# Outputs of a soft mixture of experts from C's stacked parts alone, nine first halves in one row, the last weights sent by halves

## The chip, the cores and the metric

One core of a Trainium2 chip. The metric is device time in microseconds for one execution of the whole program. Several runs of one kernel are taken and the median is given.

## The reference

The first stage is decayed block attention over `q, k, v` (4 batches, 8 heads, 768 positions, head size 64). Its result is reshaped to `x` with 3072 rows and 512 columns. The second stage is a soft mixture of 8 experts with 4 slots each, so 32 slots:

```python
logits = x @ phi                       # (3072, 32)
d = softmax of logits over the rows    # dispatch
slot_input = d.T @ x                   # (32, 512)
for e in range(8):                     # 4 slots each, F = 1024
    slot_out[e] = relu(slot_input[e] @ w1[e]) @ w2[e]
c = softmax of logits over the slots   # combine, "C" below
return c @ slot_out                    # (3072, 512)
```

All inputs and outputs are float32. The weights `w1` and `w2` are 16.8 MB each, the output is 6.3 MB.

## The kernel before, in words

The rows are cut into 24 tiles `t` of 128. In the first 110 us a loop over the tiles does the attention, the logits and the running softmax over rows, and accumulates the slots' inputs; meanwhile the weights `w1` (in "slabs" of 1 MB) and a first part of `w2` (tiles `w2t` of 256 KB, 2 KB pieces per partition) are loaded. Then the kernel closes the softmax with the last tile (lines 567 to 620), and runs the experts.

**Order.** Every engine takes its instructions in the order of the program text; a helper (line 53 of the profile) records all of them, so one line number stands for everything and groups are told apart by their tiles. All loads and outputs are issued by SyncE, one after the other, on one DMA queue.

**Experts.** `first(Q)` (lines 633 to 661) does `w1` for four experts (Q is 0 or 1): 64 matmuls into two banks, a relu on ScalarE and VectorE, then two VectorE transposes that make `hz[Q]`, the left operand of all `w2` matmuls of that Q. `second(part, ...)` (lines 676 to 690) does `w2` for one half of the contraction: 16 steps `n`, each a `quad` of 4 matmuls (8 records, because a float32 matmul runs as two passes). Steps 0 to 7 use `hz[0]`, steps 8 to 15 use `hz[1]`. `second(0)` yields the first 256 columns of the slots' outputs (the first half), `second(1)` the other 256. In `second(1)`, steps 12 to 15 use the last four units of weights (experts 4 to 7, 2 MB): steps 12 and 13 their rows with i = 0, steps 14 and 15 those with i = 1. A dictionary `fill` says before which steps other work is put in (`PUTS`, line 32).

**C.** `shares()` runs in the middle of `first(0)`. It ends the combine softmax and makes `parts`, C transposed in 32x32 blocks, as a rounded high part and a low part. `stack` (line 724) spreads these two over 128 partitions for eight tiles at a time, by 16 casts; three stacks cover the 24 tiles. Stacks 1 and 2 use ScalarE, GpSimd and VectorE in turn, stack 3 GpSimd alone. `CR` (lines 711 to 716) is a plain float32 copy of C for tiles 0 and 1.

**Outputs.** `take` copies a finished half of the slots' outputs from PSUM (first 128 columns on ScalarE, the others on VectorE). `spread` replicates it over the partitions by one matmul, and rounds it into a high and a low part (ScalarE, then VectorE on half of the partitions). `put(t, half)` makes one half of the columns for two tiles: two matmuls into one of five banks, a 128x512 copy to SBUF alternating between ScalarE and VectorE, and a DMA. For `t < 2 * SPLIT` each half is sent by itself (256 KB, 1 KB pieces); for the others one DMA of 512 KB goes after the second half. The pair t = 0 uses `CR` and needs no `spread`.

Of the kernel before, what the change touches and what calls it, by code (L numbers as in the profile page):

```python
# [8 lines left out]
F32 = mybir.dt.float32  # L9
# [5 lines left out]
P = 128  # L15
B, H, S, DH = 4, 8, 768, 64
NB = S // P
T = B * NB
HP = H // 2
D = H * DH  # L20
SL = 32
# [7 lines left out]
FS = (0, 0)  # L29
HD = D // 2  # L30

PUTS = ((2, (0, 1)), (6, (2,)), (8, (2,)), (10, (2,)))
SPLIT = 7
PACE = 76
AHEAD = 40

# [22 lines left out]
def decay_attn_soft_moe(  # L59
# [13 lines left out]
    pe, dve, act, pool, sp = (InOrder(tc, x) for x in (nc.tensor, nc.vector, nc.scalar, nc.gpsimd, nc.sync))  # L73

    const = ctx.enter_context(tc.tile_pool(name="const", bufs=1))
    slabs = ctx.enter_context(tc.tile_pool(name="slabs", bufs=NSLAB))
# [6 lines left out]
    def bank(tag):  # L83
        return ps.tile([P, 512], F32, tag=tag, name=tag)
# [17 lines left out]
    wt = {}  # L102
# [3 lines left out]
    units = [(Q, 4 * part + 2 * m, q) for part in range(2) for Q in range(2) for m in range(2) for q in range(4)]  # L106
    single = [(Q, x, q, i) for Q, x, q in units[:NONE] for i in range(2)]
    single.reverse()
    units = units[NONE:]
# [6 lines left out]
    def load_one(pool_, tag, bufs):  # L116

        Q, x, q, i = single.pop()
        t_ = pool_.tile([P, 512], F32, tag=tag, name="w2t", bufs=bufs)
        sp.dma_start(out=t_, in_=rows(Q, x, q)[i])  # L120
        wt["w2", Q, q, x, i] = t_

    def load_two():

        (Q, x, q), other = units.pop(), units.pop()
        assert other == (Q, x, q + 1)
        t_ = slabs.tile([P, 2, 2, 512], F32, tag="slab", name="w2p")
        src = w2[4 * Q + q:4 * Q + q + 2, x:x + 2].rearrange("e x p d -> e (x p d)")
        sp.dma_start(
            out=t_.rearrange("p e i d -> p e (i d)"), in_=src.rearrange("e (p y) -> p e y", p=P)  # L130
        )
        for n in range(2):
            for i in range(2):
                wt["w2", Q, q + n, x, i] = t_[:, n, i, :]
# [12 lines left out]
    half = []  # L147

    def half_slab(name):

        if not half:
            t_ = slabs.tile([P, 2, 1024], F32, tag="slab", name=name)
            half.extend([t_[:, 1], t_[:, 0]])
        return half.pop()
# [21 lines left out]
    ident = const.tile([P, P], F32, name="ident")  # L176
# [8 lines left out]
    for hh in range(2):  # L185
        for hp in range(HP):
            x = hh * HP + hp
            dve.tensor_tensor_scan(
                out=mask[:, hh, hp, :],
# [24 lines left out]
    e = const.tile([P, P], F32, name="e")  # L214
    d = const.tile([P, P], F32, name="d")
# [3 lines left out]
    AT, XT, X, ST, QS, KD = {}, {}, {}, {}, {}, {}  # L219
# [349 lines left out]
    for hp in range(HP):  # L569
        pe.matmul(  # L570
            out=pr[:, 0:P],
            lhsT=phi4[hp // 2][:, hp % 2].rearrange("p g s -> p (g s)"),
            rhs=XT[T - 1][:, hp, :],
# [8 lines left out]
    el = e  # L582
# [2 lines left out]
    wgt = small.tile([P, 1], F32, tag="alpha", name="alpha")  # L585
    act.activation(out=wgt, in_=negm, func=AF.Exp, bias=new, scale=-1.0)
    slots(G - 1)
    tr = bank("tr")
    for hp in range(HP):
        pe.transpose(tr[:, hp * P:(hp + 1) * P], XT[T - 1][:, hp, :], ident)  # L590
    xl = keep.tile([P, D], F32, tag="x", name="x", bufs=5)
    selw = small.tile([P, SL], F32, tag="selw", name="selw", bufs=1)
    act.activation(out=selw, in_=sel, func=AF.Copy, scale=wgt)
    act.copy(out=xl[:, 0:HD], in_=tr[:, 0:HD])
    dl = bank("dp")
    pe.transpose(dl[:, 0:P], el, ident)
    dn = small.tile([P, SL], F32, tag="dn", name="dn", bufs=1)
    dve.tensor_copy(out=dn, in_=dl[:, 0:SL])
    dve.tensor_copy(out=xl[:, HD:D], in_=tr[:, HD:D])

    si = bank("xa")
    for first_, (w_, x_) in ((True, (selw, acc)), (False, (dn, xl))):
        for n in range(4):
            pe.matmul(
                out=si[SL * n:SL * n + SL, 0:P].rearrange("p (i a r) -> p i a r", i=4, a=4),
                lhsT=w_,
                rhs=x_.rearrange("p (h a k r i) -> p h k i a r", h=2, a=4, k=2, i=4)[:, n // 2, n % 2],
# [25 lines left out]
    def first(Q, between=None):  # L633
        ph = [bank("gl"), bank("xb")] if Q == 0 else [bank("xa"), bank("tr")]
        split = "p (g x c) -> p x g c"
        for n in range(4):
            for j in range(2):
                for b in range(4):
                    w_ = wt["w1", Q, 2 * (b % 2) + j, n // 2][:, n % 2]
                    w_ = w_.rearrange(split, x=2, c=2 * P)[:, b // 2]  # L640
                    pe.matmul(
                        out=ph[j][SL * b:SL * b + SL, :].rearrange("p (g c) -> p g c", c=w_.shape[2]),
                        lhsT=sT[:, n, :],
                        rhs=w_,
                        start=(n == 0),
                        stop=(n == 3),
                    )
            if between is not None and n == 1:
                between()
        if Q == 1:  # L650
            hz.append(half_slab("hz").rearrange("p (a b) -> p a b", b=SL))
        h = half_slab("h").rearrange("p (j c) -> p j c", j=2)
        r_ = rown[:, 2 * Q:2 * Q + 2]
        act.activation(out=h[:, 0], in_=ph[0], func=AF.Relu, scale=r_[:, 0:1])
        dve.tensor_scalar(out=h[:, 1], in0=ph[1], scalar1=r_[:, 1:2], scalar2=0.0, op0=ALU.mult, op1=ALU.max)

        for i in range(2):
            dve.transpose(
                out=hz[Q][:, 16 * i:16 * i + 16].rearrange("p a b -> p (a b)"),
                in_=h.rearrange("p j (g r i) -> p i g j r", g=16, i=2)[:, i],  # L660
            )
# [33 lines left out]
        load_one(keep, "x", 5)  # L695
    load_one(keep, "xt", 4)
    load_one(keep, "x", 5)
    parts, CR = [], []

    def shares():  # L700

        denominators()
        lp = bank("dp")[:, 0:P]
        pe.transpose(lp, L, ident)
        for x in slot_softmax(G - 1, lp):
            pass
        for _ in range(2):
            parts.append(half_slab("part")[:, 0:T * SL].rearrange("p (t s) -> p t s", t=T))
        dve.transpose(out=parts[1], in_=CN)
        act.copy(out=parts[0].bitcast(F32R), in_=parts[1])  # L710
        CR.append(half_slab("CR")[:, 0:2 * P].rearrange("p (t c) -> p t c", t=2))
        for n in range(16):
            b, c = divmod(n, 4)
            r = slice(SL * b, SL * b + SL)
            copy = (act.copy, pool.tensor_copy, dve.tensor_copy)[n % 3]
            copy(out=CR[0][SL * c:SL * c + SL, :, r], in_=parts[1][r, 0:2, :])

    first(0, shares)
    for _ in range(4):
# [2 lines left out]
    CT, cts = [], []  # L722

    def stack(engines):

        x = len(CT)
        if x % 2 == 0:
            cts.append(slabs.tile([P, 2, 8, P], F32R, tag="slab", name="ct"))
        ct = cts[-1][:, x % 2]
        CT.append(ct)  # L730
        for n, (b, c) in enumerate((b, c) for b in range(4) for c in range(4)):
            r = slice(SL * b, SL * b + SL)
            src = parts[c % 2][r, 8 * x:8 * x + 8, :].bitcast(F32R)
            engines[n % len(engines)](out=ct[SL * c:SL * c + SL, :, r], in_=src)

    stack((act.copy, pool.tensor_copy, dve.tensor_copy))
    stack((act.copy, pool.tensor_copy, dve.tensor_copy))
    first(1)
    stack((pool.tensor_copy,))
    s4_ = cts[-1][:, 1].rearrange("p t c -> p (t c)")  # L740
    while units:
# [2 lines left out]
    so = work.tile([P, D], F32, tag="at", name="so", bufs=2)  # L744
# [3 lines left out]
    s4 = []  # L748
# [12 lines left out]
    def take(half, bank_):  # L761

        x = so[:, half * HD:(half + 1) * HD]
        act.copy(out=x[:, 0:P], in_=bank_[:, 0:P])
        dve.tensor_copy(out=x[:, P:HD], in_=bank_[:, P:HD])

    ow = {}

    def put(t, half):
        if half == 0:  # L770
            ow[t] = half_slab("o").rearrange("p (i c) -> p i c", i=2)
        o = ow[t]
        pf = bank(obanks[nput[0] % len(obanks)])
        for i in range(2):
            c_ = CT[t // 8][:, t % 8:t % 8 + 2] if t else CR[0]
            pe.matmul(
                out=pf[:, i * HD:(i + 1) * HD],
                lhsT=c_.rearrange("k t p -> k (t p)").rearrange("k (p i) -> k i p", i=2)[:, i],
                rhs=s4[half] if t else so[:, half * HD:(half + 1) * HD],
                start=True,  # L780
                stop=True,
            )
        copy = act.copy if nput[0] % 2 == 0 else dve.tensor_copy
        copy(out=o[:, :, half * HD:(half + 1) * HD], in_=pf.rearrange("p (i c) -> p i c", i=2))
        nput[0] += 1
        cols = slice(half * HD, half * HD + HD)
        if t >= 2 * SPLIT:
            cols = slice(0, D)
            if half == 0:
                return  # L790
        dst = out[t * P:(t + 2) * P, cols]
        sp.dma_start(out=dst.rearrange("(p i) c -> p i c", i=2), in_=o[:, :, cols])

    pairs = [(t, 0) for t in range(0, 2 * SPLIT, 2)] + [(0, 1)]
    pairs += [(t, 0) for t in range(2 * SPLIT, T, 2)]
    pairs += [(t, 1) for t in (*range(2 * SPLIT, T, 2), *range(2, 2 * SPLIT, 2))]
    pairs.reverse()

    def give(n):
# [10 lines left out]
    fill = {}  # L810
    for n, x in PUTS:
        fill[n] = lambda x=x: [split() if y == 0 else give(y) for y in x]
# [62 lines left out]
```

## Time and profile before

| What | Value |
|---|---|
| Median of 3 runs | 167.37 us (166.79 to 169.35) |
| Profiled execution | 167.14 us, of which the span of instructions is 165.3 us |
| Moved by DMA | 61.82 MB, mean 374 GB/s |
| Busy | TensorE 90%, VectorE 55%, GpSimd 43%, ScalarE 35% of the span |

Times in the views count from the span's start. PE is TensorE's matmul side and PEld its weight loads, DVE VectorE, ACT ScalarE, POOL GpSimd, SP SyncE. A busy PE is not PE at its peak. The DMA share is that of all 16 DMA engines together; it can read slightly over 1 in a short window, because a packet is counted where it starts.

### The profile page before, as it was taken

To read this page: it belongs to the slowest core of one execution; us is meant where nothing else is said; L and a number is where in the kernel's file an instruction comes from. 1 tells how busy PE (TensorE), PEld (TensorE's weight loads), DVE (VectorE), ACT (ScalarE), POOL (GpSimd) and SP (SyncE) were. 2 spreads that over 40 slices of the span, in tenths; PEclk is the share of its full clock that TensorE was granted. 3 is DMA by queue.
4 is the path that set the end of the run, shared out by engine and by line. 5 is a ranking of instruction groups with operands and counts; after the bars stand their busy time and mean duration, and the time that the engine had idled before them with its cause. 6 is when DMAs were issued, how large, how long until landed. Compare 5 with 4: busy or idle time off the path is not lost.

```text
span 165.3 us, 6275 instructions
## 1 busy us (share of the span) xinstructions
PE 149.1 (90%) x2651; PEld 109.0 (66%) x2651; DVE 90.3 (55%) x208; ACT 58.5 (35%) x147; POOL 71.8 (43%) x108
## 2 busy tenths in 40 slices
PE   6999999999989999999999999998999989989400
PEld 6778878677868878788868896863323455648300
DVE  2964445447744574568655775564388821328600
ACT  3134412443443444231635152242055902226400
POOL 2786790277447227766119665300022894000000
PEclk9999999999999999999999999999999999999955
DMA  5999999999999999999999999999999999982897
GB/s 165 357 418 392 312 363 414 410 423 401 412 416 402 417 409 408 410 350 344 402 415 401 415 391 394 404 390 367 375 336 396 418 416 423 396 302 76 362 402 251
DMA packets 25131, 61.82 MB, mean 374 GB/s; under 512 B 2576, under 2 KB 6288, under 8 KB 23056
## 3 DMA queue, kind: packets, MB, share of 16 engines
q1 hardware_dynamic: 24960, 61.42, 96.6%
q8 instruction: 21, 0.34, 0.7%
q14 instruction: 6, 0.05, 0.1%
q10 hardware_dynamic: 144, 0.01, 0.1%
HBM read 55.12 MB, written 6.29 MB: 371 GB/s over the span
## 4 chain that ended last, share of the span: by engine, by line
PE 66%; DVE 9%; DMA 5%; ACT 5%; POOL 4%; issue 3%; DVEq 0%; POOLq 0%; ACTq 0%
PE xa L53 17%; PE sc L53 14%; PE kv L53 10%; PE xb L53 8%; PE gl L53 8%; PE tr L53 7%; DMA w2t<-w_x 3%; DVE o L53 3%; ACT ct L53 2%; DVE mask L53 2%; DMA lam_sb<-lam_x 2%; POOL kd L53 2%; PE dp L53 2%; POOL qs L53 1%; DVE hz L53 1%
## 5 line engine op out<-in xcount | busy, mean ns | idle before, releaser
L53 DVE TENSOR_TENSOR at<-sc,mask 128x512 f32<-128x512 f32 x46 | 29.6, 685 | 15.4 <-PE sc L53 14.6
L53 ACT COPY x<-tr 128x512 f32<-128x512 f32 (+1 forms) x24 | 13.9, 578 | 37.7 <-PE tr L53 37.7
L53 POOL TENSOR_TENSOR qs<-ld,qpow 128x512 f32<-128x512 f32 x20 | 25.5, 1275 | 2.1 <-POOL kd L53 2.1
L53 PE MATMUL sc<-ld 64*64 64x128 f32 x736 | 26.0, 276 | 0.1
L53 PEld LDWEIGHTS sc<-ld 64*64 64x64 f32 x736 | 20.3, 133 | 6.2 <-issue 3.4
L53 POOL TENSOR_TENSOR dec<-st,qpow 128x256 f32<-128x256 f32 x16 | 9.9, 621 | 25.6 <-DVE st L53 25.5
L53 POOL TENSOR_TENSOR kd<-kn,mask 128x512 f32<-128x512 f32 x10 | 10.6, 1058 | 12.8 <-ACT kn L53 12.4
L53 PE MATMUL xa<-at,ld 128*64 128x128 f32 x192 | 15.8, 284 | 0.0
L53 DVE TENSOR_TENSOR st<-dec,kv 128x256 f32<-128x256 f32 x16 | 6.7, 422 | 16.5 <-PE kv L53 15.1
L53 PE MATMUL tr<-ident,xt 128*128 128x128 f32 x96 | 15.4, 283 | 0.0
L53 PE MATMUL xb<-at,ld 128*64 128x128 f32 x192 | 14.6, 273 | 0.1
L53 PE MATMUL xa<-qs,st 64*64 64x128 f32 x160 | 14.0, 274 | 0.7 <-POOL qs L53 0.3
L53 PE MATMUL xb<-qs,st 64*64 64x128 f32 x160 | 13.1, 274 | 0.6 <-issue 0.6
L53 PE MATMUL kv<-ld,kd 128*64 128x64 f32 x320 | 12.9, 223 | 0.1
L53 PEld LDWEIGHTS tr<-ident,xt 128*128 128x128 f32 x96 | 10.4, 141 | 3.8 <-issue 3.8
L53 POOL CAST ct<-part 32x256 fp32r<-32x256 f32 x26 | 10.3, 395 | 5.0 <-DVE part L53 3.9
L53 PEld LDWEIGHTS xa<-at,ld 128*64 128x64 f32 x192 | 10.0, 136 | 3.7 <-issue 1.6
L53 PEld LDWEIGHTS kv<-ld,kd 128*64 128x64 f32 x320 | 11.9, 138 | 0.8 <-issue 0.5
L53 PEld LDWEIGHTS xa<-qs,st 64*64 64x64 f32 x160 | 9.9, 133 | 3.0 <-issue 1.9
L53 PEld LDWEIGHTS xb<-at,ld 128*64 128x64 f32 x192 | 11.0, 137 | 0.3 <-issue 0.2
L53 POOL TENSOR_TENSOR kd<-ld,mask 128x512 f32<-128x512 f32 x10 | 10.6, 1059 | 0.0
L53 PEld LDWEIGHTS xb<-qs,st 64*64 64x64 f32 x160 | 9.4, 133 | 0.2 <-ACT xt L53 0.2
(148 smaller groups left out, 233.8 us busy)
## 6 DMA issues: line engine op xcount, KB each, us to landing
slab<-w_x SPq DMA_DIRECT2D x16, 1024.0 KB, 8.4
w2p<-w_x SPq DMA_DIRECT2D x10, 1024.0 KB, 10.6
ld<-qT SPq DMA_DIRECT2D x24, 256.0 KB, 6.8
ld<-kT SPq DMA_DIRECT2D x24, 256.0 KB, 6.5
ld<-vN SPq DMA_DIRECT2D x24, 256.0 KB, 7.5
w2t<-w_x SPq DMA_DIRECT2D x24, 256.0 KB, 5.4
y<-o SPq DMA_DIRECT2D x14, 256.0 KB, 4.0
ld<-kN SPq DMA_DIRECT2D x10, 256.0 KB, 7.2
```

What stands on the lines that cost most here:

```text
L53: return self._tc.keep_in_program_order(f(*args, **kwargs))
```

## The change

1. `PUTS` and `SPLIT`: in `second(1)`, `spread` of the first half stands before step 8 (was 2), and nine first halves (t = 0, 2, ..., 16) in one row before step 12 (were seven, spread over steps 2, 6, 8 and 10).
2. Nine pairs are sent by halves (were seven). The order after the last weights is (18, 0), spread of the second half, then second halves mixed with the two halves of t = 18, 20 and 22.
3. The pair t = 0 uses the stacked parts as all others do; `CR` and its 16 copies go.
4. The last four units of weights are loaded as two DMAs of 1 MB by i (pieces of 2 KB), where they were two DMAs by expert pairs (pieces of 4 KB).
5. `first(1)` stands between the first and the second stack (was after the second).
6. `take` is one ScalarE copy of 256 columns.
7. In the closing of the softmax the last tile is transposed into two banks instead of one, and the transpose of `el` is put ahead of it.

```diff
-PUTS = ((2, (0, 1)), (6, (2,)), (8, (2,)), (10, (2,)))
-SPLIT = 7
+PUTS = ((8, (0,)), (12, (9,)))
+SPLIT = 9
...
+    def load_four():
+        Q, x, _ = units[-1]
+        units.clear()
+        for i in range(2):
+            t_ = slabs.tile([P, 4, 512], F32, tag="slab", name="w2p")
+            src = w2[4 * Q:4 * Q + 4, x:x + 2].rearrange("e x p d -> e (x p d)")
+            sp.dma_start(out=t_, in_=src.rearrange("e (p i d) -> i p e d", p=P, i=2)[i])
+            for q in range(4):
+                wt["w2", Q, q, x, i] = t_[:, q]
+
     def load_two():
+        if len(units) == 4:
+            return load_four()
...
     slots(G - 1)
-    tr = bank("tr")
+    dl = bank("dp")
+    pe.transpose(dl[:, 0:P], el, ident)
+    tr = [bank(x) for x in ("tr", "sc1")]
     for hp in range(HP):
-        pe.transpose(tr[:, hp * P:(hp + 1) * P], XT[T - 1][:, hp, :], ident)
+        pe.transpose(tr[hp // 2][:, hp % 2 * P:(hp % 2 + 1) * P], XT[T - 1][:, hp, :], ident)
...
-    act.copy(out=xl[:, 0:HD], in_=tr[:, 0:HD])
-    dl = bank("dp")
-    pe.transpose(dl[:, 0:P], el, ident)
+    act.copy(out=xl[:, 0:HD], in_=tr[0][:, 0:HD])
...
-    dve.tensor_copy(out=xl[:, HD:D], in_=tr[:, HD:D])
+    dve.tensor_copy(out=xl[:, HD:D], in_=tr[1][:, 0:HD])
...
-        CR.append(half_slab("CR")[:, 0:2 * P].rearrange("p (t c) -> p t c", t=2))
-        for n in range(16):
-            b, c = divmod(n, 4)
-            r = slice(SL * b, SL * b + SL)
-            copy = (act.copy, pool.tensor_copy, dve.tensor_copy)[n % 3]
-            copy(out=CR[0][SL * c:SL * c + SL, :, r], in_=parts[1][r, 0:2, :])
...
     stack((act.copy, pool.tensor_copy, dve.tensor_copy))
+    first(1)
     stack((act.copy, pool.tensor_copy, dve.tensor_copy))
-    first(1)
     stack((pool.tensor_copy,))
...
-        act.copy(out=x[:, 0:P], in_=bank_[:, 0:P])
-        dve.tensor_copy(out=x[:, P:HD], in_=bank_[:, P:HD])
+        act.copy(out=x, in_=bank_[:, 0:HD])
...
-            c_ = CT[t // 8][:, t % 8:t % 8 + 2] if t else CR[0]
+            c_ = CT[t // 8][:, t % 8:t % 8 + 2]
...
-                rhs=s4[half] if t else so[:, half * HD:(half + 1) * HD],
+                rhs=s4[half],
...
-    pairs = [(t, 0) for t in range(0, 2 * SPLIT, 2)] + [(0, 1)]
-    pairs += [(t, 0) for t in range(2 * SPLIT, T, 2)]
-    pairs += [(t, 1) for t in (*range(2 * SPLIT, T, 2), *range(2, 2 * SPLIT, 2))]
+    pairs = [(t, 0) for t in range(0, 2 * SPLIT + 2, 2)]
+    ends = [(t, half) for t in range(2 * SPLIT, T, 2) for half in range(2)][1:]
+    for t in range(0, 2 * SPLIT, 2):
+        pairs += [(t, 1), *ends[:1]]
+        del ends[:1]
```

## Rows read from the trace of the kernel before

**Rows 1.** The page's 40 slices: busy tenths of TensorE and of the DMA engines.
```profile
PE   6999999999989999999999999998999989989400
...
DMA  5999999999999999999999999999999999982897
```

**Rows 2.** Waits, 115 to 156 us: who waited for whom, total, times, longest.
```profile
PE kv L53 <- DVE hz L53: 0.9, 1, 0.9
```

**Rows 3.** Chain of waits after 140 us: start, duration, what.
```profile
144.80 2.77 PE xa L53 x48
```

**Rows 4.** Stretches: length, busy time by engine, PE clock, DMA share, GB/s.
```profile
98.00:112.00 14.00, 13.84 (x243) 10.28 (x240) 8.44 (x27) 5.45 (x17) 4.87 (x6) 1.00 1.03 395
128.00:142.00 14.00, 13.10 (x206) 7.48 (x202) 6.39 (x13) 5.71 (x14) 9.28 (x24) 1.00 1.03 418
148.00:153.50 5.50, 5.11 (x32) 4.64 (x33) 4.09 (x8) 3.31 (x7) 0.00 (x0) 1.00 0.22 75
153.50:159.50 6.00, 1.10 (x8) 0.86 (x7) 2.09 (x4) 1.46 (x3) 0.00 (x0) 0.83 1.02 420
160.00:163.50 3.50, 0.00 (x0) 0.00 (x0) 0.00 (x0) 0.00 (x0) 0.00 (x0) 0.50 1.09 383
```

**Rows 5.** SyncE's issues in order: start, duration; last weights, then four outputs' issues.
```profile
128.16 0.43 SPq L53 DMA_DIRECT2D w2p<-w_x  x1
...
139.53 0.64 SPq L53 DMA_DIRECT2D y<-o  x1
...
150.13 0.53 SPq L53 DMA_DIRECT2D y<-o  x1
...
161.30 0.59 SPq L53 DMA_DIRECT2D y<-o  x1
```

**Rows 6.** DMA issues, the same four: KB, us from issue to landing.
```profile
w2p<-w_x SPq DMA_DIRECT2D x1, 1024.0 KB, 17.2
...
y<-o SPq DMA_DIRECT2D x1, 256.0 KB, 6.5
...
y<-o SPq DMA_DIRECT2D x1, 256.0 KB, 2.4
...
y<-o SPq DMA_DIRECT2D x1, 256.0 KB, 3.1
```

**Rows 7.** DMA queues, 143.6 to 144.6 us: packets, and those under a size.
```profile
DMA packets 362, 0.38 MB, mean 383 GB/s; under 512 B 24, under 2 KB 350, under 8 KB 362
```

**Rows 8.** Timeline, 112 to 113 us: start, duration, engine, instruction.
```profile
112.14 0.37 ACT L53 COPY x<-tr 128x256 f32<-128x256 f32 x1
...
112.55 0.42 DVE L53 COPY x<-tr 128x256 f32<-128x256 f32 x1
```

**Rows 9.** Timeline, 122 to 139 us, casts of C and the relu behind them.
```profile
122.32 1.51 ACT L53 COPY CR<-part 32x64 f32<-32x64 f32 x6
...
126.91 11.39 POOL L53 CAST ct<-part 32x256 fp32r<-32x256 f32 x26 [3.93 <-DVE part L53]
...
131.04 0.75 DVE L53 TENSOR_SCALAR hz<-tr,rown 128x512 f32<-128x512 f32 x1
```

**Rows 10.** Timeline, 136 to 144 us, matmuls of second(1) and the work put in.
```profile
136.35 1.05 PE L53 MATMUL xa<-w2p,hz 128*32 128x256 f32 x16
...
137.86 1.03 PE L53 MATMUL tr<-so,CR 128*128 128x256 f32 x4
...
142.36 0.51 PE L53 MATMUL dp<-ct 128*128 128x256 f32 x2
...
143.05 1.07 PE L53 MATMUL xa<-w2p,hz 128*32 128x256 f32 x16
```

**Rows 11.** Timeline, 147 to 151 us, what stands between the last weights and the outputs.
```profile
147.90 0.29 DVE L53 COPY so<-xa 128x128 f32<-128x128 f32 x1 [2.53 <-ACT so L53]
...
149.85 0.37 ACT L53 CAST ct<-xb 128x256 fp32r<-128x256 f32 x1 [1.99 <-PE xb L53]
...
150.12 0.59 ACT L53 COPY o<-dp 128x512 f32<-128x512 f32 x1
...
150.25 0.43 DVE L53 TENSOR_TENSOR ct<-xb,ct 64x256 fp32r<-64x256 f32 x1
```

More of the change, by code (lines that the diff above doesn't have):

```diff
@@ L697, in decay_attn_soft_moe @@
     load_one(keep, "x", 5)
-    parts, CR = [], []
+    parts = []
     def shares():
```

## The prediction, made before the changed kernel was run

> **What bounds the kernel now.** I read the page's slices first [rows 1]: TensorE and the DMA engines are both at nine tenths almost throughout, and the DMA row alone has a hole, the 2 in the fourth slice from the end. The stretches size it [rows 4]: from 148 to 153.5 us the DMA engines are busy for 0.22 of the time, so 0.78 x 5.5 = 4.3 us of transfer time is lost; before it they move 418 GB/s, behind it 420 and then 383. The end is the DMA queue's: the last output is issued at 161.30 and lands 3.1 us later, at 164.4 [rows 5, 6], 0.9 us ahead of the span's end at 165.3.
>
> The hole comes from the order of the work. The last weights land at 128.16 + 17.2 = 145.4 us [rows 5, 6]; TensorE runs its last 48 matmul records until 147.57 [rows 3]; then come take, the pair from CR, spread and its rounding [rows 11], and the queue runs dry meanwhile, with seven first halves as its only stock. After the second half of t = 0 at 150.13 five first halves follow that send nothing, hence a second dry stretch before 153.5.
>
> One more reading decides the size. Between 143.6 and 144.6 us 350 of 362 packets are under 2 KB [rows 7]: nearly all lanes of the queue already carry outputs (1 KB pieces), though the last weights land a microsecond later. A few DMA engines lag the others, and a transfer has landed only when the slowest lane has. The first output lands at 139.53 + 6.5 = 146.0 [rows 5, 6], 0.6 us behind the last weights, though it was issued 6.5 us earlier. So the slowest lane sets the end, and I count along it.
>
> **Prices on that lane.** A half of 256 KB at 383 GB/s takes 0.68 us, a whole of 512 KB at 420 GB/s 1.25 us [rows 4]. A check on before: 145.4 + 14 x 0.68 + 5 x 1.25 = 161.2 with a queue that never runs dry, and 164.4 is measured, so the hole costs this lane 3.2 us.
>
> **The change, part by part.**
>
> *Nine halves as stock, second halves mixed with the rest.* Eighteen halves and three wholes take 12.24 + 3.75 = 16.0 us, against 15.8 before: 0.2 us more. The stock of nine lasts on the slow lane until 145.4 + 9 x 0.68 = 151.5 us. The first second half must be there by then. From the last landing: 16 records of steps 14 and 15 at 2.77 / 48 each, 0.93 us [rows 3]; take as one ScalarE copy of 256 columns, 0.37 by the copy of that shape [rows 8]; the spread's matmuls, 0.6 at most (half of the float32 group of four at 1.03, and a start [rows 10]); rounding 0.37 + 0.43 [rows 11]; two matmuls 0.35, half of the 0.69 that two puts take [rows 10]; a copy of 0.59 [rows 11]; with 0.2 of hand-overs, 3.85 us. It is issued at 149.3 and lands, as a lone output does, 2.4 us later [rows 6], at 151.7; its place in the row would let it land at 152.2. It is in time by 0.5 us. Behind it the two copying engines finish a put every 0.3 us or so (0.59 on ScalarE beside a similar one), faster than 0.68. The hole on the slow lane closes: minus 3.2.
>
> *Weights by halves.* The queue then reads 2 MB in 2 KB pieces. The nearest row is the stretch from 98 to 112 us, where the w2t loads with such pieces move 395 GB/s, against 418 with 4 KB [rows 4]: 5.3 us against 5.0, plus 0.3. The other end is 0, because that stretch also holds other loads and small ones. Below nothing is excluded: larger pieces were not slower. I take 0.3, the row's own figure. In exchange steps 12 and 13 may start 2.5 us earlier than steps 14 and 15.
>
> *The nine puts in one row.* In front of step 12 they take TensorE 9 x 0.3 = 2.7 us, paced by the copies. Two puts take 0.69 where they interrupt the weights [rows 10], so 3.1 is the upper end. With the gains below, step 8 starts near 139.7 (its weights are 2 MB ahead of the last and land by 140.4 at the latest), the row at about 141.5 to 142.3, its end is at 144.3 to 145.4; steps 12 and 13 follow until 145.3 to 146.3. The lower end is hidden by the last landing at 145.7; the upper end delays the second half by 0.6, which is the margin above. SyncE issues nine sends at about 0.6 [rows 5], 5.4 us from 142.6 on, ahead of the slow lane throughout. Cost on the path 0, upper end 0.3.
>
> *CR goes, first(1) ahead of stack 2.* Now the relu of first(1) stands behind the casts on VectorE and ScalarE (131.04 [rows 9]), though its matmuls are done at about 128.5, and TensorE waits 0.9 us for hz [rows 2]. Without the CR copies (1.5 us on ScalarE [rows 9]) and with stack 2 behind it, hz comes about 2 us earlier; the wait goes, and what is late next is the weights' landing, so no more than 0.9 can be had. The pair from CR took TensorE 1.03 us [rows 10] against 0.3 now. TensorE thus reaches step 8 over 1 us earlier, but steps 14 and 15 wait for the landing at 145.4 + 0.3. These savings are cover for the row, and buy nothing by themselves. Stack 2's casts have until about 142.5; stack 3's stay on GpSimd, which does its 26 casts by 138.3 now [rows 9].
>
> *take on one engine* saves the serial 0.3 us of VectorE [rows 11] less 0.1. *The closing chain* loses the wait of VectorE's copy for ScalarE's [rows 8]; VectorE is busy with the slots' sum until shortly before, so 0.1 at best. Both lie ahead of the landing or inside the margin: 0.
>
> **Sum.** Last landing: 145.4 + 0.3 + 12.24 + 3.75 = 161.7. With the 0.9 behind it the span is 162.6, which is 165.3 - 3.2 + 0.2 + 0.3. The profiled execution takes 167.14 for a span of 165.3, so 1.84 more: **164.4 us**. Its own time is 0.2 below the median shown, which I leave.
>
> One rule speaks against sending more by halves. The rows say 0.68 us per half in a row, and so 0.2 us for four more. The Trainium skill, page "DMA: Bandwidth & Descriptors", section "Rules for kernel authors", wants at least 1 MiB per DMA, and its section "Bandwidth" gives 1 MB 78% and 64 KB 32% of the peak. By that rule the sum would grow; the 383 GB/s of the row of halves do not bear it out, and its case is the third rival.
>
> **Rivals.**
>
> 1. *The slow lane lags less, or 2 KB pieces cost nothing.* Then the common lanes decide: they idle until the first second half, which starts about 0.7 ahead of its landing at 151.7, and then need 9 x 0.68 + 3 x 1.25 = 9.9: last landing 160.9, span 161.8, time 163.6. With the lag but no price for pieces it is 164.1. For it: the lag is seen in one execution. Against: it is there at the last weights and at the first output alike. Chance 0.32.
> 2. *The hole is moved, not closed.* If TensorE comes to steps 14 and 15 late (row of nine at its upper end, a bank held by a copy) or VectorE is held at the (18, 0) copy in front of the rounding, each microsecond past the 0.5 of margin is lost: one to two of them give 165.4 to 166.4. Against: 0.9 + 0.7 us of TensorE's own savings. Chance 0.10.
> 3. *Small sends do not overlap.* A lone half takes 2.4 us; if four halves cost 4 x 2.4 = 9.6 where two wholes cost 2 x (2.4 - 0.68 + 1.25) = 5.9, that is 3.7 in place of 0.2: 167.9. The page named above would put it so. Against: fourteen halves already follow each other at 383 GB/s. Chance 0.03.
> 4. *The load by halves is slow, and the kernel slower.* The last two DMAs gather 2 KB pieces of four experts. At half the rate (209 GB/s) 2 MB take 10.0 us, 5 more: everything behind moves, and 164.1 becomes 169.1. It is slower than before once the rate falls below 2.1 MB / (5.0 + 3.0) us = 260 GB/s, and by 2% below some 190. Against: w2t has such pieces at 395 [rows 4]. Chance 0.05.
>
> **Numbers.** The forecast has 0.50, in 164.0 to 164.9. Two per cent, about what a measurement of this kernel can tell from no change, is 3.3 us, so 164.0 on the median and just under 163.9 on the profiled execution: the line cuts through rival 1 and touches the forecast. Faster: 0.27 of rival 1 and 0.10 of the forecast, 0.37. Slower: 0.04, nearly all of rival 4. Same: 0.59. The range of 162.9 to 166.2 takes in rival 1 with some gain on top and rival 2; it leaves out rivals 3 and 4.
>
> **What would show it.** Right: DMA share near 1 from 143 to about 161 us on the slow lane, a dip on the others of well under 2 us near 150; halves landing 0.7 us apart; TensorE waiting for w2p in front of step 14 and no longer for hz; last weights landing at 145 to 146. Wrong: a stretch without outputs after 148 (rival 2), weights landing after 147 (rival 4), halves over 0.8 us apart (rival 3), or weights and outputs landing without a lag (rival 1).

## The result, and the profile after

The changed kernel takes 166.23 us in the median of 22 runs, against 167.74 for 22 runs of the kernel before. The ratio is 0.990, interval 0.988 to 0.993: 1% faster, where 164.4 us and about 1.7% were forecast. Ratios leave out runs over 1.5% above the fastest of the same kernel, here among them one of 474.51 us. The profiled execution takes 166.88 us, with a span of 165.0.

The stretches behind the last weights first (columns as in [rows 4]), and below them the longest one in the kernel before.

```profile
142.50:145.00 2.50, 2.50 (x21) 2.05 (x16) 1.36 (x3) 1.57 (x3) 0.00 (x0) 1.00 0.22 85
149.00:150.50 1.50, 0.96 (x8) 0.96 (x9) 0.60 (x2) 0.44 (x2) 0.00 (x0) 1.00 0.49 168
142.50:154.00 11.50, 10.15 (x87) 7.54 (x82) 7.28 (x13) 7.31 (x14) 0.00 (x0) 1.00 0.79 284
```

```profile
142.50:154.00 11.50, 10.64 (x107) 7.95 (x108) 6.08 (x11) 5.23 (x11) 0.00 (x0) 1.00 0.63 226
```

The old hole from 148 to 153.5 [rows 4] is nearly gone: what is left of it is half a share between 149 and 150.5. But a new one stands in front of it. From 142.5 to 145 us the DMA engines are busy for 0.22 of the time, where the kernel before was already sending outputs [rows 7]. Over the whole stretch the idle time fell from 0.37 x 11.5 = 4.3 us to 2.4.

SyncE's issues of the changed kernel tell why, with start and duration, the last weights first and then the first, third, fourth, seventh, tenth and last output (read as [rows 5]).

```profile
128.32 4.02 SPq L53 DMA_DIRECT2D w2p<-w_x  x1
...
144.01 0.64 SPq L53 DMA_DIRECT2D y<-h  x1
...
145.39 0.59 SPq L53 DMA_DIRECT2D y<-o  x1
...
146.08 0.59 SPq L53 DMA_DIRECT2D y<-o  x1
...
148.10 1.54 SPq L53 DMA_DIRECT2D y<-o  x1
...
151.08 0.59 SPq L53 DMA_DIRECT2D y<-h  x1
...
159.51 0.58 SPq L53 DMA_DIRECT2D y<-o  x1
```

The same issues from start to landing, in the same order (read as [rows 6]).

```profile
w2p<-w_x SPq DMA_DIRECT2D x1, 1024.0 KB, 18.0
...
y<-h SPq DMA_DIRECT2D x1, 256.0 KB, 3.0
...
y<-o SPq DMA_DIRECT2D x1, 256.0 KB, 3.0
...
y<-o SPq DMA_DIRECT2D x1, 256.0 KB, 4.6
...
y<-o SPq DMA_DIRECT2D x1, 256.0 KB, 4.6
...
y<-h SPq DMA_DIRECT2D x1, 256.0 KB, 3.6
...
y<-o SPq DMA_DIRECT2D x1, 256.0 KB, 4.4
```

The first output goes out at 144.01, 4.5 us later than before (139.53 [rows 5]). From then on a half follows each 0.67 us or so, just the pace at which the queue drains, so that no stock is built. The first output lands at 147.0, 0.7 us behind the last weights at 146.3: the lane that set both had no hole, the others had. The third output lands at 148.4, the fourth at 150.7, 2.3 us later in place of 0.68; this document calls such a step the **jump**. The second half of t = 0 is issued at 151.08.

TensorE's part of it is in the chain of waits of the changed kernel (start, duration, what).

```profile
125.75 15.20 DMA w2p<-w_x
140.96 0.04 issue
141.00 1.92 PE xa L53 x28
142.92 0.44 PE tr L53 x2
...
145.56 1.91 PE xa L53 x32
147.47 0.02 issue
147.49 0.38 ACT so L53
...
147.91 0.71 PE xb L53 x2
...
148.65 0.38 ACT ct L53
...
149.06 0.44 DVE ct L53
...
149.54 0.51 PE tr L53 x2
```

Step 8 waits for its weights until 140.96; the row of nine starts at 142.92 only and ends at 145.5; steps 12 to 15 end at 147.47. The wait for hz [rows 2] is gone, and the waits (who for whom, total, times, longest) now show weights in its place:

```profile
PE xa L53 <- DMA w2p<-w_x: 0.8, 1, 0.8
```

One number serves below to compare profiles: the **drain**, from the landing of the last weights to that of the last output. It is free of what happens in the first 140 us, which moves single executions by up to 2 us. Before it is 164.4 - 145.4 = 19.0 us, after 163.9 - 146.3 = 17.6, and the forecast's sum holds 16.0 (12.24 + 3.75).

### The profile page after: what moved, and what is told of

Its sections match the earlier page's. It is cut to its first block, busy times and chain, and to the rows that moved or that the text cites. A ratio compares the mean times of both kernels' runs of the same rounds, so it can differ in the third digit from the quotient of the medians.

```text
span 165.0 us, 6250 instructions
## 1 busy us (share of the span) xinstructions
PE 147.9 (90%) x2647; PEld 108.1 (66%) x2647; DVE 88.3 (54%) x201; ACT 57.1 (35%) x141; POOL 70.6 (43%) x103
## 4 chain that ended last, share of the span: by engine, by line
PE 70%; DMA 11%; DVE 5%; POOL 4%; issue 2%; ACT 0%; DVEq 0%; SPq 0%; POOLq 0%
PE xa L53 17%; PE sc L53 14%; PE xb L53 10%; PE gl L53 10%; DMA w2p<-w_x 9%; PE tr L53 9%; PE kv L53 8%; DVE o L53 2%; DVE mask L53 2%; DMA lam_sb<-lam_x 2%; PE dp L53 2%; POOL kd L53 2%; POOL qs L53 2%; POOL phi_sb L53 1%; DVE acc L53 0%
## 5 line engine op out<-in xcount | busy, mean ns | idle before, releaser
L53 DVE TENSOR_TENSOR st<-dec,kv 128x256 f32<-128x256 f32 x16 | 6.7, 421 | 16.4 <-PE kv L53 15.0
L53 ACT COPY xt<-xa 128x256 f32<-128x256 f32 x24 | 8.8, 369 | 2.0 <-PE xa L53 1.8
```

The costliest lines, as they stand in the source:

```text
L53: return self._tc.keep_in_program_order(f(*args, **kwargs))
```

## The experiments

Each ratio is to the kernel before, with its interval; times of the kernels of one group were taken beside each other. The theories: **A**, one DMA engine that lags sets the end; **B**, the stock of outputs comes too late; **C** and **D** were formed on the way, C that the parts 3 to 7 carry the gain, D that both are true, because the row before step 12 opens a hole as large as the one it closes.

### First group: where the missing microsecond is

The changed kernel as a control.

> The changed kernel as it is, beside which the others of this group are read. Both theories: about 1% faster than before, 166.2 us, spread of its runs some 2 us. Theory A (slow lane): what is missing of the forecast is one DMA engine that lags; in the profile the last weights land 3 us after the other engines have finished theirs, and outputs land at even steps of 0.68 us with a jump of over 1 us where a 16 KB instruction block is fetched. Theory B (late stock): the first output is issued at 144.0 only, all engines but the slow one stand idle from 142.6 to 145.1, and that hole is what is missing.

Measured: 0.989 (0.985 to 0.993), drain 165.7 - 148.3 = 17.4 us. Outputs land each 0.68 us with one jump of 2.2 us, as A said, and the first is issued when nearly all lanes of the queue have stood idle for 2 us, as B said.

The row earlier:

```diff
-PUTS = ((8, (0,)), (12, (9,)))
+PUTS = ((2, (0,)), (8, (9,)))
```

> The changed kernel with spread of the first half before step 2 and the row of nine before step 8, where TensorE waits for weights anyway; the first output is then issued near 141, before the common engines have finished their weights at 142.6. Theory B: the hole of 2.5 us goes and the time falls by about 1.5 to 2.0 us, to 164.5. Theory A: the slow engine has no hole there now, so the time stays within 0.4 us of the control, though the hole of the others goes.

Measured: 0.984 (0.979 to 0.989), by the ratios 0.9 us under the control (the medians lie 1.3 apart); drain 162.4 - 146.3 = 16.1 us. That is outside A's 0.4 us and short of B's 1.5 to 2.0. The two intervals still touch; the third group repeats the run.

One more block of instructions behind the last put:

```diff
+    idle = bank("gl")
+    for _ in range(64):
+        pe.matmul(out=idle[0:SL, 0:4], lhsT=ident[:, 0:SL], rhs=ident[:, 0:4], start=True, stop=True)
```

> The changed kernel with 64 tiny matmuls (two passes each, 256 instructions, one block of 16 KB) behind the last put, when TensorE is idle; they write a bank that nobody reads. They cost no time on any path but the fetch of one more block of instructions while the outputs drain. Theory A: the engine that fetches ends 0.7 to 1.6 us later, and so does the kernel: 167 to 167.8. Theory B: the common engines end last, no change (within 0.3 us).

Measured: 0.993 (0.990 to 0.996), 0.4% above the control's ratio, with intervals that overlap (the medians of all runs lie 0.07 us apart), so the times alone leave A's lower end open. The profile decides more: the block was fetched near 158 us, the outputs behind it land 0.68 and 1.25 us apart as in the changed kernel, and the drain is 163.8 - 146.2 = 17.6 us. In this execution the added fetch cost the end nothing, so A's cost of 0.7 to 1.6 us for each fetch is not borne out.

Five second halves in two DMAs:

```diff
+        if half and t < 10:
+            sp.dma_start(out=dst[0:120], in_=o[0:120, :, cols])
+            sp.dma_start(out=dst[120:P], in_=o[120:P, :, cols])
+            return
```

> The changed kernel with five of the second halves sent as two DMAs, of partitions 0 to 119 and 120 to 127, which by the Trainium skill (DMA: Bandwidth & Descriptors, section on why a DMA increments its semaphore by 16) run on 15 and on 8 of the 16 engines, so that the sixteenth carries 80 KB less and the first eight 10 KB more. Theory A: if the slow engine is the sixteenth, it ends 3 us earlier, the common ones set the end, and the kernel is 1.0 to 1.3 us faster than the control; if it is one of the first eight, 0.4 us slower; between them unchanged. Theory B: 0.1 us slower at most, apart from the five extra issues on SyncE, which have room.

Measured: 1.000 (0.996 to 1.004), slower than the control by 1%. It doesn't answer its question. The stretch from 151 to 161 us, this kernel's:

```profile
151.00:161.00 10.00, 2.00 (x14) 1.68 (x13) 2.98 (x5) 2.36 (x5) 0.00 (x0) 0.80 0.77 251
```

The control's:

```profile
151.00:161.00 10.00, 4.08 (x28) 3.71 (x28) 4.70 (x8) 4.20 (x8) 0.00 (x0) 0.90 1.03 382
```

The small pieces cost SyncE as much issue time as whole halves, and the queue ran dry between them: the experiment changed the pace of the sends, not only their place. Which engine lags was not found out.

### Second group: which part of the change carries what

Parts 1 and 2 alone, that is the kernel before with the new `PUTS`, `SPLIT` and order of pairs:

```diff
-PUTS = ((2, (0, 1)), (6, (2,)), (8, (2,)), (10, (2,)))
-SPLIT = 7
+PUTS = ((8, (0,)), (12, (9,)))
+SPLIT = 9
...
+    pairs = [(t, 0) for t in range(0, 2 * SPLIT + 2, 2)]
```

> The kernel before with parts 1 and 2 of the change alone: the row of nine before step 12, nine pairs by halves and the mixed order of the second halves; CR, the loads, the casts and the rest as before. Theory B (late stock: the first output waits for the row, and SyncE then sends one half each 0.67 us, as fast as the queue drains, so that no stock is built): most of the change's gain is here, 0.5 to 1% faster than before, within 0.6 us of the changed kernel. Theory C (the other parts carry the gain): not faster than before, as the first output goes out 3 us later than in the kernel before.

Measured: 1.001 (0.997 to 1.004). Nothing, as C said. Its first output is issued at 145.28, and this is the stretch behind the weights, with the whole one beside it:

```profile
144.50:146.50 2.00, 2.00 (x16) 1.87 (x15) 1.59 (x3) 1.81 (x4) 0.00 (x0) 1.00 0.03 12
142.50:154.00 11.50, 11.17 (x102) 8.51 (x94) 6.29 (x13) 6.13 (x12) 0.00 (x0) 1.00 0.69 247
```

For 2 us the queue is all but empty, for every engine this time: the first output lands 2.4 us behind the last weights, 1.7 more than in the changed kernel. The drain is 164.8 - 145.4 = 19.4 us, longer than the 19.0 before: one hole was traded for another.

Parts 3 to 7 alone, that is the changed kernel with the old sends:

```diff
-PUTS = ((8, (0,)), (12, (9,)))
-SPLIT = 9
+PUTS = ((2, (0,)), (6, (3,)), (8, (2,)), (10, (2,)))
+SPLIT = 7
...
+    pairs = [(t, 0) for t in range(0, 2 * SPLIT + 2, 2)] + [(0, 1)]
+    pairs += [(t, 0) for t in range(2 * SPLIT + 2, T, 2)]
+    pairs += [(t, 1) for t in (*range(2 * SPLIT, T, 2), *range(2, 2 * SPLIT, 2))]
```

> The changed kernel with the sends of the kernel before: seven first halves (three before step 6, two before 8, two before 10, spread before step 2), seven pairs by halves and the old order of the second halves, save that (14, 0) stands ahead of (0, 1) to cover the spread; parts 3 to 7 of the change stay. Theory B: the hole behind the last weights is as in the kernel before, where the queue holds nothing; parts 3 to 7 shorten the chain in front of the second halves by 1 us, so 0.3 to 0.6% faster than before. Theory C: as fast as the changed kernel, 0.9% or more.

Measured: 0.989 (0.985 to 0.994): by this ratio the whole gain of the change, as C said. It is less firm than the interval looks: the median of all twelve runs, 167.11 us, is only 0.4% under the 167.83 of the kernel before beside it. Its stretches:

```profile
142.50:145.00 2.50, 2.50 (x32) 1.56 (x29) 0.80 (x2) 0.59 (x1) 0.00 (x0) 1.00 1.05 396
149.50:153.50 4.00, 3.02 (x20) 2.52 (x20) 2.61 (x5) 2.14 (x6) 0.00 (x0) 1.00 0.19 62
```

No hole in front, the old one behind. The drain is 165.7 - 148.0 = 17.7 us. From the last landing to the first second half's issue it takes 4.4 us (152.38) against 4.7 before, and to the issue after it 5.9 (153.92) against 7.3 (152.66). TensorE is done 1.1 us after the landing (149.14 in its chain), before 2.2.

The last weights by expert pairs again:

```diff
-        if len(units) == 4:
-            return load_four()
```

> The changed kernel with the last four units of weights loaded as two DMAs by expert pairs, in pieces of 4 KB, as before. By the forecast's price the last weights land 0.3 us earlier, and steps 12 to 15 all wait for them, which puts the second halves 0.7 us later: since SyncE is still busy with the row of nine then, theory B says no change, within 0.4 us of the changed kernel. If the pieces of 2 KB or the longer issue (4 us on SyncE) were what costs the missing 1.3 us, it is 0.8 to 1.5 us faster than the changed kernel.

Measured: 0.991 (0.988 to 0.995), the changed kernel's ratio. Neither the 2 KB pieces nor SyncE's long issue of them (4.02 us at 128.32) is what is missing.

Half a block more of TensorE's instructions at the start:

```diff
+    for _ in range(32):
+        pe.matmul(out=wps[0:SL, 0:4], lhsT=warm[:, 0:SL], rhs=warm[:, 0:4], start=True, stop=True)
```

> The changed kernel with 32 tiny matmuls (128 instructions, half a block of 16 KB) at the very start, where TensorE waits for its first data; they write a bank that is written again later. They move the moments at which TensorE's instruction blocks are fetched by half a block, the last one from 148 to about 143 us. Theory A (one engine delayed by the fetch throttles the sends): the jump of 2.3 us between the landings of the third and fourth output is gone, outputs land each 0.68 us, and the time is 0.5 to 1.5 us under the changed kernel's unless the weights land later by as much. Theory B: the jump may move, the median stays within 0.4 us.

Measured: 1.018 (1.012 to 1.024). The tiny matmuls were not free: TensorE's first transposes start at 6.44 us instead of 4.30, and the last weights land 1.6 us later than in the changed kernel. That is not all of the 4.9 us by which the ratios put it behind the control; the rest stays unexplained. The last block is fetched at 148.7, 0.8 us behind the landing of the last weights, where the control's is 1.7 behind: it moved by 0.8 us against the weights, not by the 5 expected. The jump has moved with it, from between the third and fourth output to between the first and second. The drain is 165.8 - 147.9 = 17.9 us. So the jump goes with the fetch in time, but the time was not bought back.

### Third group: the row's place, with and without the other parts

The earlier row once more, as the reference.

> The row of nine before step 8 once more, as the reference of this group. Theory D (the row at step 12 opens a hole of 2 to 3 us behind the weights, as large as the one it closes; parts 3 to 7 alone carry the change's 1%; the earlier row closes both): 1.4 to 1.9% faster than before.

Measured: 0.984 (0.979 to 0.989). The stretches (again two), and the first and last output:

```profile
142.50:145.00 2.50, 2.32 (x44) 1.16 (x40) 0.00 (x0) 0.00 (x0) 0.00 (x0) 1.00 1.03 369
142.50:154.00 11.50, 8.37 (x88) 5.74 (x80) 5.39 (x9) 4.64 (x9) 0.00 (x0) 1.00 0.95 343
```

```profile
140.32 0.64 SPq L53 DMA_DIRECT2D y<-h  x1
...
157.62 0.58 SPq L53 DMA_DIRECT2D y<-o  x1
```

The first output is issued while the weights still move, the share stays at 0.95, the jump is 0.2 us, and the drain is 160.8 - 144.7 = 16.1 us: the forecast's 16.0.

Parts 1 and 2 alone, with the row before step 8:

```diff
-PUTS = ((8, (0,)), (12, (9,)))
+PUTS = ((2, (0,)), (8, (9,)))
```

> The kernel before with parts 1 and 2 alone, the row of nine being put before step 8 and the spread before step 2. Theory D: the first output goes out near 142 instead of 145.3, the hole behind the weights is gone and the one at 150 is nearly closed, so 0.5 to 1.0% faster than before, where the same row before step 12 gave nothing. Theory C (the sends don't matter, only the shorter chain does): no faster than before.

Measured: 0.990 (0.986 to 0.994), drain 162.5 - 145.0 = 17.5 us. The same sends that gave nothing before step 12 give 1% before step 8. That refutes C in its strict form and bears out D.

The row before step 4:

```diff
-PUTS = ((8, (0,)), (12, (9,)))
+PUTS = ((1, (0,)), (4, (9,)))
```

> The changed kernel with the spread before step 1 and the row of nine before step 4, 2 us earlier still. Theory D: the queue is full of weights until 142.6 anyway, so no further gain, within 0.3% of the row before step 8. If SyncE's pace of one half each 0.67 us were what limits the drain, the sooner start would be worth up to 1 us more.

Measured: 0.981 (0.976 to 0.986), not to be told from the row before step 8. SyncE's pace is not what is left. The profiled execution has a jump all the same, 2.1 us between the landings of the fifth and sixth output, and a drain of 163.1 - 145.8 = 17.3 us: the early row doesn't rule the jump out.

All twelve pairs by halves:

```diff
-PUTS = ((8, (0,)), (12, (9,)))
-SPLIT = 9
+PUTS = ((2, (0,)), (8, (9,)), (12, (3,)))
+SPLIT = 12
```

> The changed kernel with the row of nine before step 8, the other three first halves before step 12, and all twelve pairs by halves: second halves alone behind the last weights. The stock is 8.2 us instead of 6.1, which closes the common engines' hole at 150 to 152 of the row before step 8. If the common engines set the end, 0.5 to 1.0 us faster than that kernel; if the slowest engine does, which has no hole there, no faster, or 0.2 us slower for three more pieces.

Measured: 0.990 (0.984 to 0.995), drain 162.5 - 146.1 = 16.4 us, with hardly any idle time between 142.5 and 154:

```profile
142.50:154.00 11.50, 9.44 (x100) 6.44 (x98) 6.23 (x11) 5.75 (x12) 0.00 (x0) 1.00 1.04 371
```

A nearly full queue (a full one of halves reads 1.09, last line of [rows 4]), and yet no gain over the kernel with 0.95: the idle time of the common engines (all but the slow one) at 150 costs nothing there, and three more pieces cost about what was reckoned (16.3 for 24 halves at 0.68). Its median is higher than the reference's by more than that; the intervals overlap, and it was not followed up.

The combinations in one table (ratio, and the drain of one execution each):

| | sends as before | row before step 12 | row before step 8 |
|---|---|---|---|
| other parts as before | 1, 19.0 us | 1.001, 19.4 us | 0.990, 17.5 us |
| parts 3 to 7 | 0.989, 17.7 us | 0.990, 17.6 us | 0.984, 16.1 us |

## Why the prediction was wrong

**The reading of before was right.** The end is the DMA queue's, the hole behind the last weights costs it 3 us, and a queue that never runs dry drains in 16.0 us: with the row before step 8 it does, in 16.1. The forecast of 164.4 us is, in effect, that of this kernel: 165.2 and 164.5 in its two groups.

**The step that failed** is the cost of the nine puts in one row, "cost on the path 0, upper end 0.3", with SyncE sending "from 142.6 on, ahead of the slow lane throughout". Measured, the first send goes out at 144.01, and moving the same nine puts ahead of step 8 is worth about 1 us (0.984 in both groups against 0.990). One term of that step was wrong too: the weights of step 8, "land by 140.4 at the latest", land at 140.96, and the row begins at 142.92 in place of 142.3 at the latest. I checked the row against the last weights' landing, where TensorE has time to spare, and not against the moment at which the queue has nothing left, which for most engines is about 142.6. The stock has to be there at that moment. By my own bounds the row could begin as late as 142.3, and its first copy and issue come 1.1 us behind (142.92 to 144.01), so even they gave a hole; I had priced it along the slow lane alone, where it is hidden. Before, seven halves were issued from 139.53 on, and the row took that stock away in order to make another. The table shows the price: parts 1 and 2 gained 0 before step 12, and 1% before step 8.

**The second miss is the other side of the same step.** TensorE's savings (CR, the wait for hz, take) were said to "buy nothing by themselves". By the ratio they bought all of the 1%: without the row, parts 3 to 7 give 0.989 (by the median of all runs less, as said above), and TensorE then ends 1.1 us behind the landing instead of 2.2, and the second halves follow sooner. In the kernel before TensorE was behind the weights, not waiting for them; I had turned "landing is next" into "no gain", though the chain of before had 2.2 us behind the landing, and 1.1 of it could go.

**Along the slow lane** the sum was too small by two terms in this execution. The last weights land at 146.3, forecast 145.7. And between the third and fourth output 2.3 us pass, not 0.68: 1.6 us, just what lies between the drain of 17.6 and 16.0. The forecast had no such term. So in this execution the hole in front, which spared the lane that ends last, did not lengthen the drain by itself; what the late row costs shows only in the comparison of times. SyncE's issue at 148.10 took 1.54 us at the same time; which of the two made the other is not shown. With the nine sends out earlier the jump was 0 to 0.2 us more than 0.68 in three executions (row8, row8b, all12), 1.4 in row4 and 1.6 in sends8.

**Right in mechanism and size:** the wait for hz went, and weights took its place; halves land 0.68 us apart and wholes 1.25, so that 1 KB pieces cost little (the row of the trace against the Trainium skill's rule of at least 1 MiB, page "DMA: Bandwidth & Descriptors", section "Rules for kernel authors": the trace does not agree with it here, as long as sends overlap). The price of loading by halves is within noise. **The rivals:** the second, the hole moved and not closed, came true, but 6 us ahead of where I looked for it, and with a chance of 0.10; its time, 165.4 to 166.4, holds the result. The first had two halves: the lag was there, and whether 2 KB pieces cost nothing can't be told from 0.3 us within the noise. The third and fourth did not happen.

**Open:** what decides whether the jump comes. It follows the fetch of TensorE's last instruction block in each of the eight profiles that have it (the last section), but the same fetch without a jump stands in four others, and an added fetch cost nothing. So how the late row turns into lost time is not shown; that it does, is.

## What to carry to other kernels

When work is gathered into one block to fill a queue later, look at the moment at which the queue runs dry, and whether what was taken away from it there is worth more than what is put in. Price the savings of an engine against the chain behind the last transfer, not only against the transfer. And try the place of a block separately from its content: the same nine sends gave 0 or 1% four steps apart.

## What was not expected of the hardware

A fetch of TensorE's instructions goes over the same DMA engines as the data, as one packet of 16 KB (21 of them in the control, 22 with the 64 tiny matmuls behind the last put); this is the line of the queues of the changed kernel from 148.1 to 148.3 us (packets, MB, share).

```profile
q8 instruction: 1, 0.02, 33.2%
```

In eight profiles (after, ctrl, fetch, pairs, sends, sends8, shift, row4) one output lands 1.9 to 2.7 us behind the one ahead of it, each time the first to land after such a fetch ended, 1.3 to 1.6 us behind its end; in before, row8, row8b and all12 a fetch at the same place of the program is followed by at most 0.9. (In rest the fetch falls into the hole, and k15's landings are not all in its trace.) The Trainium skill, page "Runtime: NRT & Kernel Launch", section "Instruction fetch mechanics", has the blocks of 16 KiB and calls the cost of crossing one mostly hidden. In the first eight the trace doesn't look so, in the other four it does.

The packets of sends show how one fetch can hold up a landing. Its queue had been empty, so the engines started level: 16 of the small packets that end an engine's share for each of the first two outputs. After the fetch at 148.07 there are 15 for each of the next two, and then this, from 149.46 to 150.47 us.

```profile
DMA packets 17, 0.02 MB, mean 16 GB/s; under 512 B 1, under 2 KB 17, under 8 KB 17
```

Those are 16 packets of 1 KB and one that ends them, one engine's share of one output: one engine works alone, the third output lands at 150.95, and 1.8 us are lost. If an engine is well ahead of the slowest when the fetch comes to it, such a delay would not be seen at a landing; and a hole, in which engines idle until they are level, takes that lead away. That would tie the late row to the jump, but it is argued, not shown: no run changed the lead alone, and the jump of row4 came without a hole in front.
